# Tiles 4 and 5 of the first feed-forward turned by VectorE and through device memory, with a new order

## The chip, the cores and the metric

The program runs on one core of a Trainium2 chip. Its engines are TensorE (PE; its weight loads are shown as PEld), VectorE (DVE), ScalarE (ACT), GpSimd (POOL) and SyncE (SP, which here issues most of the transfers). The metric is the time of one execution on the device in microseconds (us).

## The reference

Attention, then two feed-forwards, all in fp32, on 4 x 576 = 2304 tokens of width 512:

```python
B, H, S, D = 4, 8, 576, 64                      # attention
scores = q @ k.T / sqrt(D), masked where (pos_q // 64) < (pos_k // 64)
attn = softmax(scores);  x = attn @ v           # heads joined: 2304 x 512
h = x @ w_in                                    # 512 -> 1024
solu = h * softmax(h)
ln = (solu - mean) / sqrt(var + 1e-6) * g_ln    # over the 1024
x = ln @ w_out                                  # 1024 -> 512
h = x @ w2_in                                   # 512 -> 2048
g = h * tanh(log1p(exp(h)))
out = g @ w2_out                                # 2048 -> 512
```

## The kernel before

All products keep fp32 accuracy by splitting each operand into a high and a low part and adding three products (high x high, high x low, low x high). L345 and L348 make a high part on ACT or POOL, L351 and L354 the low part on DVE or POOL.

**Attention** (`pair`, L639) works in 16 pairs of heads, four pairs to a batch. For a pair PE makes the scores (L792), DVE the maxima (L828, L854), ACT the exponentials with their sums (L812), POOL the division by the sum (L868, "norms": ten instructions, two heads times five blocks of queries, pt0 to pt4), PE the transposes of the result (L885), DVE and ACT the copies of these out of PSUM (L891, L894), PE the product with v (L906, L913, "pv").

**The first feed-forward** (`moe1_tile`, L951) works in 18 tiles of 128 tokens, 9 groups of two, woven between the pairs from the second batch on. POOL splits the tile's x into a high and a low part (L348, L354), with two buffers of each. PE makes h with 24 matmuls (L980), in four steps of six. DVE takes the maximum (L1005), ACT the exponentials (L1007), DVE the product (L1012), ACT the squares (L1017), POOL the layer norm (L1023, L1025) into e, of which there are three. The second product wants the tile with its 1024 features on the partitions, and there are two ways to get it:

- Plain: PE makes 8 transposes into PSUM (L1040), ACT the high part lth from PSUM (L345), DVE the low part ltl (L351).
- Turned (`moe1_turn`, L1050): DVE transposes e within blocks of 32x32 (L1060), SP stores it to device memory (L1061) and reads it back into ltl so that the blocks change places (L1064); then ACT makes lth and DVE ltl, both from SBUF.

There is one lth and one ltl, each with a half for either tile of a group. The group's second product (`moe1_x2`, L1072) is 96 matmuls (L1078), then ACT copies it out of PSUM (L1095) and SP stores it (L1098). Weights are scaled and split on the way by all engines (L469 to L527).

**The second feed-forward** (L1261 to L1522) does three groups of 768 tokens, with part of its blocks combined so that fewer products are needed (L1281, L1373, L1405), from about 390 us on.

**The order** of each engine's queue is planned when the program is built, by a list scheduler (`Plan`, L95). Every operation has an estimated cost, the operations it depends on, and a due time, which is `base + step * i` out of the table PRIO for its kind and the number of its tile or pair; an engine that is free takes the operation ready by the estimate with the lowest due time. Tiles from 6 on have due times of their own, of the names that end in "_z" (L942). The eight banks of PSUM are given out in the same plan. An entry of `ends` (L1093) makes a tile's first step of L980 wait in the plan for the second product three groups earlier.

Of the kernel before, what the change touches and what calls it, by code (L numbers as in the profile page):

```python
# [16 lines left out]
AF = mybir.ActivationFunctionType  # L17
# [22 lines left out]
    "m_x": (3584561924, 4.740681981), "m_h": (3584519723, 224.5432339), "m_v": (3578365590, -84.55132086),  # L40
    "m_w": (3584549757, 31.61235543), "m_u": (3578776343, 462337.2769), "m_s": (3583814990, 14.58923958),
    "m_l": (3584293716, 224.7120364), "m_t": (3584285833, 15.52739263), "m_e": (3584649368, -15732.34345),
    "m_2": (3584549910, 3.263592163), "m_o": (3584964114, -730.4305853),
    "store": (58386273008.57153, -19416.76233711018), "load_k_b": (2099539261, 66301361.76),
    "load_q_b": (2280296400, -83.7998511), "load_v_b": (3584392328, -36.03664193), "tr_b": (3573582281, 115.1413154),
    "te_b": (3583493493, 70.21914347000001), "sc_b": (3584300715, -653.4032456), "mx_b": (3574374210, 834066.0729),
    "ex_b": (3573775268, 127599.6585), "su_b": (3578364250, 29.19757548), "nm_b": (3584435794, 211661.1709),
    "pt_b": (3578363557, 165.0890833), "pe_b": (3584395710, -341.7218587), "pv_b": (3584415435, -2.221819743),
    "po_b": (3584391454, 26.30453126), "f_x": (58390434490.2532, 1768.025953882861),
    "f_t": (58371420326.68462, 3135.361618856386), "f_s": (3584428469.415521, 4.026125945181665),  # L50
    "f_h": (58390429881.5704, 1955.565874337728), "f_c": (3583099578.05821, 33.34836585602606),
    "f_d": (3584434386.986156, -235.5845758800226), "f_v": (58371478114.65918, 316.375216701946),
    "f_a": (58370115856.04984, 57586.70997751181), "f_pa": (58389724266.28586, 11.24711881543841),
    "f_pb": (3605493742.834323, -937869.0345814368), "f_qa": (58371450659.66384, 403.297702353877),
    "f_qb": (58371282887.06215, 12127.04963138201), "f_oa": (58380321299.68896, 492616.8487495577),
    "f_ob": (58386515692.55923, 64046.06512203981), "f_ea": (58387500502.18478, 27343.66933933209),
    "f_eb": (58389243067.357, 31275.66497336231), "f_ga": (3584428449.271045, 4.026125945181665),
    "f_gb": (58371476723.55054, 113.1749626307466), "w2c": (58392108169.53233, 419.4872966149516),
    "w2cr": (3601350414.022446, -762901.4270400213), "w2p": (3599949210.25516, -1918829.73352),
    "w2q": (58390522316.82204, -82311.19795111436), "w2br": (3588491921.201982, -390526.3022309779),  # L60
    "w2b": (58371421877.10077, 978.8919243511407), "f_p": (58385293999.53715, 95352.01411378416),
    "f_q": (3583103160.04437, 2541.501991236126), "f_o": (3583019597.915153, -19416.76233711018),
    "f_e": (3572968236.729074, 1136300.372042182), "f_b": (58383687706.18044, 5.384888595012861),
    "f_p1": (58389906945.48666, 1914.35193605864), "f_q1": (3582481840.635309, 64046.06512203981),
    "f_o1": (3582978577.934009, -22.66799827023639), "f_e1": (58390440550.8709, 33.34836585602606),
    "f_gc": (3584434234.266353, -235.5845758800226), "f_pc": (3576948007.906397, 376573.2326307783),
# [6 lines left out]
    "m_o_z": (58386217914.21704, 4407.161850113993), "m_s_z": (58391201631.55981, -768559.3758905744),
    "m_t_z": (58393876313.12167, -610611.3720098342), "m_u_z": (58383670558.39252, 1294.017841619403),
    "m_v_z": (58392113639.12505, 189.399987384369), "m_w_z": (3622369903.655326, -3465318.056893601),
    "m_x_z": (3584795119.264935, 49.97933876348363), "m_y_z": (3584428441.267128, 4.355726728622709),
}
# [224 lines left out]
def kernel(  # L302
# [58 lines left out]
    def ps(s):  # L361
        return banks[s.at // 2][:, s.at % 2, :]
# [276 lines left out]
    def pair(p, xt):  # L639
# [1028 lines left out]
```

## Time and profile before

| | us |
|---|---|
| runs | 760.08, 760.74, 761.40 |
| median | 760.74 |
| profiled execution | 761.4 |
| its span | 759.6 |
| PE busy | 749.1 |
| DVE busy | 574.4 |
| ACT busy | 443.2 |
| POOL busy | 253.3 |

The span is the time from the first to the last instruction that the profiler recorded; 1.8 us lie around it. Busy times are sums over instructions of an engine. Matmuls overlap one another, so what PE spends on a row of them is read from the start of the first to the start of the next other instruction, not from the mean duration.

### The profile page before, as it was taken

Reading aid. Unit: us, or ns where it says so; the run is one execution under the profiler, and the core shown is the slowest. Engines: PE = TensorE matmul, PEld = TensorE weight load, DVE = VectorE, ACT = ScalarE, POOL = GpSimd, SP = SyncE. Lnnn points to the kernel's source line nnn. Section 1 sums busy time; section 2 is a strip of 40 time slices with the busy share of each in tenths; the row PEclk is TensorE's granted clock in tenths of the full one; section 3 lists DMA queues with packets and bytes.
Section 4 is the critical chain, followed back from the end, with each engine's and each line's share of the span. In section 5 each row is a group of like instructions: output and inputs, shape, how many; then the busy total and the mean of one; then the engine's idle time right before and its main releaser. Section 6 shows DMA issues by size and latency. Waiting matters only on the chain.

```text
span 759.6 us, 14749 instructions
## 1 busy us (share of the span) xinstructions
PE 749.1 (99%) x5490; PEld 682.7 (90%) x5490; DVE 574.4 (76%) x1187; ACT 443.2 (58%) x936; POOL 253.3 (33%) x299
## 2 busy tenths in 40 slices
PE   8999999999999999999999999999999999999998
PEld 6888888788888899999998989989988999999998
DVE  6989888999997999978833868752334579569995
ACT  5998897686766565544723745554455555354560
POOL 2687877784674333543410242210000000000000
PEclk9999999999999999999999999999999999999999
DMA  7764653336335376658664676772287561282303
GB/s 189 181 152 106 153 129 98 98 83 171 122 115 188 98 242 197 210 186 313 243 218 163 246 263 217 251 283 99 80 291 228 169 250 59 95 302 73 98 1 111
DMA packets 114023, 128.58 MB, mean 169 GB/s; under 512 B 64160, under 2 KB 81824, under 8 KB 113952
## 3 DMA queue, kind: packets, MB, share of 16 engines
q1 hardware_dynamic: 113536, 127.35, 52.5%
q8 instruction: 43, 0.70, 0.4%
q10 hardware_dynamic: 416, 0.30, 0.1%
q14 instruction: 28, 0.23, 0.1%
HBM read 81.48 MB, written 46.14 MB: 168 GB/s over the span
## 4 chain that ended last, share of the span: by engine, by line
PE 89%; DVE 7%; ACT 2%; issue 1%; POOL 1%; DVEq 0%; ACTq 0%
PE ps L1281 23%; PE ps L1405 13%; PE ps L1078 12%; PE ps L1373 12%; PE ps L980 10%; PE ps L792 5%; PE ps L885 5%; PE ps L906 5%; PE ps L913 1%; PE ps L728 1%; DVE nmx L854 1%; DVE ltl L351 1%; PE ps L1040 1%; ACT pt L812 1%; POOL pt L868 1%
## 5 line engine op out<-in xcount | busy, mean ns | idle before, releaser
L1281 PE MATMUL ps<-wk,w2ih 128*128 128x384 f32 x576 | 146.7, 336 | 0.0
L868 POOL TENSOR_SCALAR pt<-pt,sm 128x576 f32<-128x576 f32 (+4 forms) x160 | 93.6, 605 | 32.0 <-ACT pt L812 14.1
L1281 PEld LDWEIGHTS ps<-wk,w2ih 128*128 128x128 f32 x576 | 102.7, 188 | 1.0
L980 PE MATMUL ps<-wk 128*128 128x512 f32 x432 | 103.3, 394 | 0.0
L1281 PE MATMUL ps<-wk,w2il 128*128 128x384 f32 x288 | 96.9, 336 | 0.0
L980 PEld LDWEIGHTS ps<-wk 128*128 128x128 f32 x432 | 79.6, 188 | 17.1 <-issue 1.1
L812 ACT ACTIVATE pt<-ps,nmx 128x192 f32<-128x192 f32 (+4 forms) x160 | 81.7, 525 | 20.3 <-DVE nmx L854 13.5
L1078 PE MATMUL ps<-lth,woh 128*128 128x256 f32 x288 | 82.3, 286 | 0.0
L1078 PE MATMUL ps<-ltl,woh 128*128 128x256 f32 x288 | 81.5, 283 | 0.6 <-DVE ltl L351 0.5
L1078 PE MATMUL ps<-lth,wol 128*128 128x256 f32 x288 | 81.6, 283 | 0.0
L527 POOL TENSOR_TENSOR wem<-wem 128x512 f32<-128x512 f32 x40 | 54.6, 1367 | 62.7 <-DVE wem L524 31.9
L1405 PE MATMUL ps<-w2oh,cl 128*128 128x512 f32 x144 | 56.2, 390 | 0.3 <-DVE cl L351 0.3
L1078 PEld LDWEIGHTS ps<-ltl,woh 128*128 128x128 f32 x288 | 54.3, 188 | 1.3 <-DVE ltl L351 0.7
L1373 PE MATMUL ps<-w2oh,cl 128*128 128x256 f32 x196 | 55.2, 282 | 0.0
L1078 PEld LDWEIGHTS ps<-lth,woh 128*128 128x128 f32 x288 | 54.3, 188 | 1.0 <-issue 0.5
L1078 PEld LDWEIGHTS ps<-lth,wol 128*128 128x128 f32 x288 | 54.2, 188 | 0.0
L1281 PEld LDWEIGHTS ps<-wk,w2il 128*128 128x128 f32 x288 | 54.1, 188 | 0.0
L885 PE MATMUL ps<-ident,pt 128*128 128x128 f32 (+1 forms) x400 | 51.4, 276 | 1.1 <-DVE kl L351 0.6
L885 PEld LDWEIGHTS ps<-ident,pt 128*128 128x128 f32 (+1 forms) x400 | 45.4, 142 | 6.4 <-issue 2.5
L354 POOL TENSOR_TENSOR wk<-xf,wk 128x768 fp32r<-128x768 f32 x9 | 21.1, 2339 | 71.0 <-ACT wk L345 65.7
L854 DVE TENSOR_REDUCE nmx<-ps 128x2 f32<-128x896 f32 (+1 forms) x64 | 40.7, 679 | 5.3 <-PE ps L792 3.5
L906 PE MATMUL ps<-ptw,vraw 128*64 128x256 f32 (+1 forms) x384 | 38.1, 348 | 0.0
(195 smaller groups left out, 1937.4 us busy)
## 6 DMA issues: line engine op xcount, KB each, us to landing
blk_d<-wk SPq DMA_DIRECT2D x36, 384.0 KB, 3.6
wk<-blk_d SPq DMA_DIRECT2D x36, 384.0 KB, 5.7
wraw<-in_moe_w_in_dram SPq DMA_DIRECT2D x24, 512.0 KB, 4.3
park_d<-wem SPq DMA_DIRECT2D x20, 448.0 KB, 2.8
wraw<-in_moe_w_out_dram SPq DMA_DIRECT2D x16, 512.0 KB, 4.2
wem<-park_d SPq DMA_DIRECT2D x18, 448.0 KB, 4.3
lT_d<-e SPq DMA_DIRECT2D x10, 512.0 KB, 3.2
ltl<-lT_d SPq DMA_DIRECT2D x10, 512.0 KB, 4.8
```

What stands on the lines that cost most here:

```text
L527: add(POOL, c_tt(wd), lambda: nc.gpsimd.tensor_tensor(out=mf(), in0=mf(), in1=ex().bitcast(F32), op=ALU.mult), r=[ek], w=[mk], **pt)
L792: nc.tensor.matmul(out=dst[:R1(t)], lhsT=a_[hs, (t + 1) * P - R1(t):(t + 1) * P], rhs=m_[hs, o + c0:o + c1], start=(i == 0), stop=(i == 2 ...
L812: add(ACT, c_act(EXT[t], acc=True), lambda: nc.scalar.activation(out=pp.t[0:R1(t), x * EXT[t]:(x + 1) * EXT[t]] if t < 4 else pp.t[:, x * ...
L854: add(DVE, 2 * c_dve(512), lambda s=s, ts=ts: [nc.vector.tensor_reduce(out=nmx.t[0:R1(t), :, t], in_=ps2(s)[0:R1(t), :, o:o + EXT[t]], axi ...
L868: nc.gpsimd.tensor_scalar(pp, pp, sm.t[0:R1(t), x, t:t + 1], 1.0, op0=ALU.mult, op1=ALU.mult)
L885: nc.tensor.transpose(ps2(s)[:, a, o + P - n:o + P], pts[t].t[0:n, c * P:(c + 1) * P], ident[0:n, 0:n])
L906: nc.tensor.matmul(out=ps(os_[r])[x * D:(x + 1) * D, o:o + n_], lhsT=vr.t[:, j, x, :], rhs=packs[pi].t[:, a, c0:c0 + n_], start=(i in (0, ...
L980: nc.tensor.matmul(out=ps2(hp)[:, hf, :], lhsT=x.t[:, kk, :], rhs=w[:, kk, hf * 512:(hf + 1) * 512], start=bool(first), stop=bool(last))
L1078: nc.tensor.matmul(out=ps(s)[:, (c % 2) * 256:(c % 2) * 256 + 256], lhsT=w[:, kk, cs], rhs=x.t[:, :, :, kk, :].rearrange("p o a j -> p (o ...
L1281: nc.tensor.matmul(out=ps(s)[:, 0:HT], lhsT=sl_i[j, w][:, c, a, :], rhs=x.t[:, mv], start=(start and c == 0 and i == 0), stop=(c == 1 and ...
L1373: nc.tensor.matmul(out=ps(acc[bi])[:, h * 256:(h + 1) * 256], lhsT=x.t[:, a], rhs=sl_o[j, w][:, b], start=(first and h == 0 and y == 0), s ...
L1405: nc.tensor.matmul(out=ps(acc[t]), lhsT=x.t[:, 2 * t + f], rhs=plain(j, w, f), start=(first and f == 0 and y == 0), stop=(last and f == 1 ...
```

## The change

Tiles 4 and 5, which were plain, are turned (`TURNED = range(4, 16)`), so that 12 tiles are turned and tiles 0 to 3, 16 and 17 are plain. The due times with names in "_z" hold from tile 4 on. An entry of `ends` is made from group 1 on, so that the tiles of group 4 wait in the plan for the second product of group 1. Nearly all due times from "wor" on have new numbers, of which the diff below shows one. The conditions with `p < 99` are true for every pair (p goes to 15), so with them the same copies run on the same engines.

```diff
@@ -35,45 +35,49 @@ PRIO
...
-    "wi": (3584443192, 7.799761221), "wor": (3586624350, -34.01260267), "wo": (3584561778, 29.75716834),
...
+    "wi": (3584443192, 7.799761221), "wor": (6008160774.962386, 25.39232252916657),
...
@@ -887,7 +891,7 @@
-            if pi == 1:
+            if pi == 1 and p < 99:
...
@@ -917,13 +921,13 @@
-            if r:
+            if r and p < 99:
...
-                add(ACT, c_act(w), lambda c0=c0, w=w: nc.scalar.activation(
-                    out=xt.t[:, h2, c0:c0 + w], in_=ps(os_[0])[:, 0:w], func=AF.Copy), r=[oks[0]], w=[xks[0]],
-                    rel=[os_[0]], prio=pri("po", p))
+                add(ACT, c_act(w), lambda r=r, c0=c0, w=w: nc.scalar.activation(
+                    out=xt.t[:, h2, c0:c0 + w], in_=ps(os_[r])[:, 0:w], func=AF.Copy), r=[oks[r]], w=[xks[r]],
+                    rel=[os_[r]], prio=pri("po", p))
...
@@ -940,9 +944,9 @@
     def mpri(tag, i):
-        return pri(tag + ("_z" if i >= 6 else ""), i)
-
-    TURNED = range(6, 16)
+        return pri(tag + ("_z" if i >= 4 else ""), i)
+
+    TURNED = range(4, 16)
...
@@ -1090,7 +1094,7 @@
-            if g >= 3 - 1:
+            if g >= 2 - 1:
                 ends[g] = o.seq
```

By count the new program has 48 transposes at L1040 where before has 64, 12 instead of 10 of L1060, and 12 instead of 10 of each of the transfers of L1061 and L1064; every other kind has the same number. What moves is shown below at three places. Lines of after are four higher than the same lines of before (L885 is L889, L1078 is L1082 and so on).

PE, end of the transposes of the last pair (pt0_1 is the block of queries 0 of one of its heads; ident the identity; e1, e2 tiles 4 and 5; vraw1 the pair's v). Before:

```order
L885 MATMUL ps2_65<-ident_67,pt2_1_119 128x128
L885 MATMUL ps2_65<-ident_67,pt1_1_117 128x128
L885 MATMUL ps2_65<-ident_67,pt0_1_115 128x64
L1040 MATMUL ps0_63<-ident_67,e1_147 128x128 x8
L1040 MATMUL ps3_66<-ident_67,e2_148 128x128 x8
L906 MATMUL ps1_64<-ptw0_124,vraw1_101 64x256 x2
L906 MATMUL ps1_64<-ptw1_125,vraw1_101 64x128 x2
```

After:

```order
L889 MATMUL ps1_64<-ident_67,pt3_1_121 128x128
L889 MATMUL ps1_64<-ident_67,pt2_1_119 128x128
L889 MATMUL ps1_64<-ident_67,pt1_1_117 128x128
L889 MATMUL ps1_64<-ident_67,pt0_1_115 128x64
L1082 MATMUL ps3_66<-lth0_155,woh_90 128x256
L1082 MATMUL ps3_66<-ltl0_156,woh_90 128x256
L1082 MATMUL ps3_66<-lth0_155,wol_91 128x256
```

The sixteen transposes of e1 and e2 are gone, and behind the pair's last transpose stands the second product of group 2 (lth0, ltl0) where pv stood.

ACT, what makes the high parts of tiles 4 and 5 (lth0; ptw are copies of the transposed pt out of PSUM). Before:

```order
L1095 ACTIVATE xo1_88<-ps2_65 128x512
L894 ACTIVATE ptw0_124<-ps3_66 128x1024
L894 ACTIVATE ptw2_126<-ps2_65 128x896
L345 ACTIVATE lth0_155<-ps0_63 128x8x4x32
L345 ACTIVATE lth0_155<-ps3_66 128x8x4x32
L492 ACTIVATE ps0_63<-wem1_95 128x512
L924 ACTIVATE xt1_145<-ps1_64 128x320
```

After:

```order
L816 ACTIVATE pt3_0_120,sm0_139<-ps1_64,nmx0_137 128x448 x2
L816 ACTIVATE pt0_0_114,sm0_139<-ps1_64,nmx0_137 64x64 x2
L816 ACTIVATE pt1_0_116,sm0_139<-ps3_66,nmx0_137 128x192 x2
L349 ACTIVATE lth0_155<-ltl0_156 128x1024
L816 ACTIVATE pt2_0_118,sm0_139<-ps3_66,nmx0_137 128x320
L349 ACTIVATE lth0_155<-ltl0_156 128x1024
L816 ACTIVATE pt2_0_118,sm0_139<-ps3_66,nmx0_137 128x320
L928 ACTIVATE xt1_145<-ps0_63 128x320
```

The two high parts now read ltl0 and not PSUM, and stand between the exponentials of pair 14 (pt2_0), where they stood behind the last copies of the last pair.

POOL, norms of pair 14 (pt0_0 to pt4_0) and of pair 15 (pt0_1 to pt4_1), with wk the buffers of the split x. Before:

```order
L1023 TENSOR_TENSOR st2_152<-st2_152,edges_72 128x1
L1025 TENSOR_SCALAR e0_146<-e0_146,st2_152 128x1024
L868 TENSOR_SCALAR pt4_1_123<-pt4_1_123,sm1_140 128x576 x2
L868 TENSOR_SCALAR pt3_1_121<-pt3_1_121,sm1_140 128x448 x2
L868 TENSOR_SCALAR pt2_1_119<-pt2_1_119,sm1_140 128x320 x2
L868 TENSOR_SCALAR pt1_1_117<-pt1_1_117,sm1_140 128x192 x2
L868 TENSOR_SCALAR pt0_1_115<-pt0_1_115,sm1_140 64x64 x2
L527 TENSOR_TENSOR wem1_95<-wem1_95 128x512
L348 TENSOR_SCALAR wk_89<-xt0_144 128x512
L354 TENSOR_TENSOR wk_89<-xt0_144,wk_89 128x512
```

After:

```order
L872 TENSOR_SCALAR pt0_0_114<-pt0_0_114,sm0_139 64x64 x2
L352 TENSOR_SCALAR wk_89<-xt0_144 128x512
L358 TENSOR_TENSOR wk_89<-xt0_144,wk_89 128x512
L872 TENSOR_SCALAR pt4_1_123<-pt4_1_123,sm1_140 128x576 x2
L872 TENSOR_SCALAR pt3_1_121<-pt3_1_121,sm1_140 128x448 x2
L872 TENSOR_SCALAR pt2_1_119<-pt2_1_119,sm1_140 128x320 x2
L872 TENSOR_SCALAR pt1_1_117<-pt1_1_117,sm1_140 128x192 x2
L872 TENSOR_SCALAR pt0_1_115<-pt0_1_115,sm1_140 64x64
L1027 TENSOR_TENSOR st0_150<-st0_150,edges_72 128x1
L872 TENSOR_SCALAR pt0_1_115<-pt0_1_115,sm1_140 64x64
```

The split of a tile of x (tile 10 after) now stands ahead of the norms of pair 15, and an instruction of a layer norm (st0) ahead of the last of them; before, two splits followed behind the norms and a weight product.

## Rows read from the trace of the kernel before

**Rows 1.** Head of the page: the span, busy us by engine.
```profile
span 759.6 us, 14749 instructions
...
PE 749.1 (99%) x5490; PEld 682.7 (90%) x5490; DVE 574.4 (76%) x1187; ACT 443.2 (58%) x936; POOL 253.3 (33%) x299
```

**Rows 2.** PE's waits: line, releaser, us in total, times, longest.
```profile
PE ps L728 <- ACT pt L812: 1.6, 2, 1.4
...
PE ps L1078 <- DVE ltl L351: 0.5, 1, 0.5
```

**Rows 3.** Two stretches: length, busy us of each engine, granted clock, DMA.
```profile
125.00:245.00 120.00, 119.82 (x1061) 101.64 (x1060) 110.47 (x228) 81.82 (x187) 79.76 (x102) 1.00 0.44 130
410.00:760.00 350.00, 346.06 (x2106) 328.96 (x2104) 229.76 (x519) 175.95 (x333) 26.82 (x14) 1.00 0.51 175
```

**Rows 4.** PE in time: start, us, line, operation, count, [idle before].
```profile
241.02 2.99 PE L885 MATMUL ps<-ident,pt 128*128 128x128 f32 x25
243.94 1.97 PE L1040 MATMUL ps<-ident,e 128*128 128x128 f32 x16
245.83 2.38 PE L906 MATMUL ps<-ptw,vraw 128*64 128x256 f32 x24
...
389.89 1.91 PE L1040 MATMUL ps<-ident,e 128*128 128x128 f32 x16
391.56 0.60 PE L1281 MATMUL ps<-wk,w2ih 128*128 128x384 f32 x2
```

**Rows 5.** The turned path's instructions by shape: busy us, mean ns, idle before.
```profile
L1060 DVE STREAM_TRANSPOSE e<-e 128x1024 f32<-128x1024 f32 x10 | 12.3, 1233 | 0.0
L351 DVE TENSOR_TENSOR ltl<-ltl,lth 128x1024 fp32r<-128x1024 f32 x10 | 12.2, 1248 | 0.0
...
L345 ACT ACTIVATE lth<-ltl 128x1024 fp32r<-128x1024 f32 x10 | 10.5, 1055 | 7.5 <-DMA ltl<-lT_d 7.5
```

**Rows 6.** The reads at L1064, from issue to landing.
```profile
DMA to landing us min/median/max: 3.8/4.8/6.5
```

**Rows 7.** All engines in time around the last pair's scores and norms.
```profile
225.81 0.47 PE L792 MATMUL ps<-kh,qh 64*128 64x448 f32 x2
...
227.62 2.38 PE L906 MATMUL ps<-ptw,vraw 128*64 128x256 f32 x24
...
229.95 0.63 ACT L812 ACTIVATE pt<-ps,nmx 128x448 f32<-128x448 f32 x1 [3.00 <-DVE nmx L854]
...
230.67 1.29 PE L885 MATMUL ps<-ident,pt 128*128 128x128 f32 x9
...
233.46 0.21 ACT L812 ACTIVATION_READ_ACCUMULATOR pt<-ps,nmx 128x1 f32 x1
...
234.51 6.21 POOL L868 TENSOR_SCALAR pt<-pt,sm 128x576 f32<-128x576 f32 x10 [5.19 <-ACT ptw L894]
```

**Rows 8.** Chain that ended last, in time: start, us, line, count.
```profile
333.13 11.52 PE ps L1078 x96
344.64 10.91 PE ps L980 x48
```

**Rows 9.** POOL's instructions by shape: busy us, mean ns, idle before.
```profile
L527 POOL TENSOR_TENSOR wem<-wem 128x512 f32<-128x512 f32 x40 | 54.6, 1367 | 62.7 <-DVE wem L524 31.9 <-DVE wem L512 27.6 <-DVE sm L806 2.0
...
L1023 POOL TENSOR_TENSOR st<-st,edges 128x1 f32<-128x1 f32 x18 | 12.7, 706 | 39.2 <-DVE st L1020 30.6 <-ACT pt L812 4.4 <-DVE st L1010 4.1
L348 POOL TENSOR_SCALAR wk<-xt 128x512 fp32r<-128x512 f32 x16 | 11.6, 726 | 34.1 <-PE ps L980 34.1
L868 POOL TENSOR_SCALAR pt<-pt,sm 64x64 f32<-64x64 f32 x32 | 11.0, 355 | 0.0
```

**Rows 10.** POOL in time, one split of x.
```profile
265.80 0.63 POOL L348 TENSOR_SCALAR wk<-xt 128x512 fp32r<-128x512 f32 x1
266.51 1.30 POOL L354 TENSOR_TENSOR wk<-xt,wk 128x512 fp32r<-128x512 f32 x1
```

**Rows 11.** SP's queue in time, its longest stand at issues.
```profile
401.11 6.12 SPq L1098 DMA_DIRECT2D x_d<-xo  x2
```

More of the change, by code (lines that the diff above doesn't have):

```diff
@@ L37 @@
     "pv": (3577602489, 48250.73415), "po": (3584548697, -23973.45369), "wir": (3584391592, -19.40282866),
[2 rows of a table removed]
[L40 to L66, printed above, removed]
@@ L67 @@
-    "f_qc": (58383687262.01283, 13.38236390586725), "f_oc": (58389948370.77222, 292.4769573812346),
-    "f_ec": (58391600633.60854, 28506.90281875799), "m_f": (3584285833, 15.52739263),
-    "m_g": (3584649368, -15732.34345), "m_y": (3584285833, 15.52739263),
-    "m_2_z": (3584411683.580256, 1158.898595520469), "m_e_z": (3583097759.795254, 93.04242884762695),
-    "m_f_z": (3576036552.304828, 925082.38871505), "m_g_z": (58383687409.47991, 1.493118386126717),
-    "m_h_z": (3584421142.964115, 529.2117548921229), "m_l_z": (58390132850.49834, -24266.92028098213),
@@ L73 @@
[L73 to L76, printed above, removed]
[3 rows of a table added]
+    "m_h": (4146513034.229027, 3437.496074077945), "m_v": (1685692734.528723, 70908.15921127236),
@@ new lines @@
+    "m_w": (3513359135.780956, 44.92415547201797), "m_u": (3512651070.661022, 34412.19942918024),
+    "m_s": (3602385031.112902, 229.5407375045089), "m_l": (3512621139.104277, 48.91441027733243),
+    "m_t": (3606374493.707211, 57176.39760572281), "m_e": (3784256872.698033, 46580.35398076692),
+    "m_2": (5814751679.425178, 28.5543752261172), "m_o": (4154032517.959847, 50721.31479615544),
+    "store": (3784480023.569042, 13636.80493405584), "load_k_b": (3513412592.897239, 18.28911371657496),
@@ new lines @@
+    "load_q_b": (3591457380.578043, 5455.750659667706), "load_v_b": (5814747705.540405, 37.91630800520451),
+    "tr_b": (3513512623.624942, 2488.864339361115), "te_b": (3513057446.15823, 20449.54855869562),
+    "sc_b": (3598471054.04015, -12660.51456856392), "mx_b": (4146460362.438111, 4956.416609931926),
+    "ex_b": (3513202159.696492, 278.2843291448102), "su_b": (3512973138.696665, 30410.34632864956),
+    "nm_b": (5982003734.634109, 6084678.409851378), "pt_b": (3512517669.298651, 67677.18311275712),
@@ new lines @@
+    "pe_b": (3512467939.144368, 83173.24540044068), "pv_b": (3606497905.709489, 90.00238067856172),
+    "po_b": (3513385991.199829, 26.56050018958916), "f_x": (6008156650.597215, 779.5970689903637),
+    "f_t": (3512610350.138847, 297.2943001073333), "f_s": (3513379921.223451, 4443.91599878809),
+    "f_h": (4154435668.646057, 4366.717098724009), "f_c": (3512037548.931818, 110873.3650727735),
+    "f_d": (3589689352.875807, 100987.1606545643), "f_v": (3513530414.556408, 161.5853800552079),
+    "f_a": (3598525495.763744, 170280.8380340209), "f_pa": (6034878513.585733, -14655.90053063708),
@@ new lines @@
+    "f_pb": (3602385031.112902, 229.5407375045089), "f_qa": (3842060795.519964, 530797.0666234276),
+    "f_qb": (3784481313.98589, 13636.80493405584), "f_oa": (-34603326918.33231, 1916686514.745709),
+    "f_ob": (3512607912.105052, 515.2284187708756), "f_ea": (4148351975.506439, 251384.4518498256),
+    "f_eb": (3513326696.170582, 293.7535488451618), "f_ga": (-4661520550.137727, -21372.20211791259),
+    "f_gb": (3602413546.967874, 149.3463499252079), "w2c": (6008154478.291977, 699.1231476218337),
@@ new lines @@
+    "w2cr": (3513152301.192077, 12933.16787216247), "w2p": (3512786932.347193, 43329.16647657341),
+    "w2q": (4146479428.070339, 278.1596871225091), "w2br": (3513354402.041589, 185.2169332069646),
+    "w2b": (3513357920.996052, 2648.217017198866), "f_p": (3784450968.790502, 5197.830628909945),
+    "f_q": (6008153046.339516, 897.8736645491898), "f_o": (3513194028.87609, 26801.98206807588),
+    "f_e": (6008160178.324902, 229.5407375045089), "f_b": (3513404899.396112, 16.29491305222635),
+    "f_p1": (5814751385.815626, 24.38853313023387), "f_q1": (3511641561.398437, 104369.5322552285),
@@ new lines @@
+    "f_o1": (3602283256.191959, 1416131.234380976), "f_e1": (3512914070.688581, -21774.17885624363),
+    "f_gc": (3512409399.332546, -37.78460661017908), "f_pc": (5814751203.764366, 37.88205393319141),
+    "f_qc": (3513354402.041589, 185.2169332069646), "f_oc": (3591426039.129261, 6190.879925856177),
+    "f_ec": (6034648267.007865, 95.66622213876178), "m_f": (3584285833, 15.52739263),
+    "m_g": (3584649368, -15732.34345), "m_y": (3584285833, 15.52739263),
+    "m_2_z": (4142659699.299991, 284285.4825035536), "m_e_z": (3512611608.553393, 574.706807828762),
@@ new lines @@
+    "m_f_z": (1685692385.457383, 70908.27551583681), "m_g_z": (3512574052.685516, 6014.459998772267),
+    "m_h_z": (5814751173.256117, 38.1373011500683), "m_l_z": (4154203218.34231, 29332.82787552609),
+    "m_o_z": (5806522791.316294, 630850.4569228797), "m_s_z": (3511815669.800803, 85067.1320595883),
+    "m_t_z": (3605651132.16607, 52408.33006597407), "m_u_z": (3854040242.696799, 1540.748222960061),
+    "m_v_z": (4167864452.473848, 75.48390070549195), "m_w_z": (3513270665.232864, 38393.04278283695),
@@ L77 @@
+    "m_x_z": (3784923448.291461, 625.3016034869008), "m_y_z": (3512553666.470055, 361.3495936685188),
 }
```

3 rows, old and new, of the table PRIO are left out of this document.

## The prediction

> **What bounds the kernel now.** I began with the page's head: TensorE (PE) is busy 749.1 of a span of 759.6 us [rows 1]. A busy PE can still wait between matmuls, so next came PE's waits: the longest that belongs to the first feed-forward is 0.5 us, the largest group of all 1.6 us [rows 2]. Then the stretches: between 125 and 245 us, where tiles 4 and 5 are worked beside the last attention pairs, PE is busy 119.8 of 120 us, VectorE (DVE) 110.5 and GpSimd (POOL) 79.8 at full granted clock; after 410 us the second feed-forward has PE at 346.1 of 350 and DVE at 229.8 [rows 3]. So the time is the number of matmuls in PE's queue, and an edit pays what it takes out of that queue, less the waits it puts in. The other engines matter where a result comes just in time.
>
> The profiled execution took 761.4 us (759.6 of span, 1.8 around it); the median of the runs shown is 760.74. I work with differences against the profiled one and take them off the median.
>
> **Part 1: the transposes that go.** Sixteen of PE's 64 transposes at L1040 belong to tiles 4 and 5. The trace has just these 16: they start at 243.94 and the next matmuls at 245.83, so 1.89 us, of which 0.15 is the change to another kind of matmul; 16 others took 389.89 to 391.56, 1.67 us; and the 25 transposes ahead of the first lot took 2.92 us, 0.117 each [rows 4]. I take 16 x 0.109 = **-1.74** (bounds -1.67 and -1.89). None of it lies beside other PE work.
> The Trainium skill speaks against the edit here: in "VectorE: DVE Perf Modes", section "The three transpose paths", TensorE is the path to use for 128x128 when the result may lie in PSUM, at 390 ns each. By that price 16 would be 6.2 us (an estimate from that page) and the time 754.5; the rows price all 16 in a row, so they decide.
>
> **Part 2: what replaces them.** Per tile: one DVE transpose of 1.23 us, one store and one read of 512 KB, a high part on ScalarE (ACT) of 1.06 us and a low part on DVE of 1.25, where the old path has the same two parts from PSUM [rows 5]. So only the DVE transposes and the transfers are new: DVE has 9.5 us to spare in the stretch and gets 2.5 more. The reads land 3.8 to 6.5 us after issue [rows 6]. They may start only when the product of group 1 (tiles 2, 3) is done, because there is one pair of buffers lth, ltl. Call that moment zero. PE's new queue has from there to the product of group 2: scores of 24 matmuls, pv, 6 of L980, 8 transposes, 12 of L980, 17 transposes. Scores take 1.81 and pv 3.05 [rows 7]; a matmul of L980 is 10.91/48 = 0.227 and one of L1078 11.52/96 = 0.120 [rows 8]. The sum is 1.81 + 3.05 + 1.36 + 0.87 + 2.72 + 1.85 = 11.7 us. The second read, issued 0.4 after the first, lands by 6.9 at the worst of the rows; 1.06 and 1.25 later all is ready, at 9.2. So I cost the round trip at nothing, with 2.5 us of cover (bounds 0 to 1: a stretched DVE instruction and one softmax exponential on ACT first do not use the cover up). What is queued behind the wait: on ACT, which now stands at the first lth in the middle of pair 14's exponentials, one exponential, the second lth and another exponential; pair 14's sums and POOL's norms wait for those. PE's next transposes of that pair come 11.7 + 1.44 + 1.0 + 4.32 = 18.5 us after zero (12 products, a half run of scores, 36 products). The norms end about 15.4: the second lth at 8.0, an exponential and the sums to 9.2 (1.2 is an estimate), ten norms in 6.21 [rows 7].
>
> **Part 3: the order of the last pair.** Here I see a cost. Before, the last pair's scores end at 227.62, the exponentials run from 229.95 to 233.67, POOL's ten norms 234.51 to 240.72, PE's transposes start at 241.02 [rows 7]: 13.4 us of cover, all but 0.3 used. After, PE has between the same two points pv, 6 of L980, 9 transposes, 12 of L1078, pv, 12 of L1078: 3.05 + 1.36 + 1.0 + 1.44 + 3.05 + 1.44 = 11.3 us, and the last 9 of the 25 transposes follow 1.8 later, at 13.1. And POOL now stands ahead of the norms at tile 10's splits (L348, L354 of before), which write a buffer that tile 8's last 6 matmuls read: L348 is the line that waits 34.1 us for L980 in the trace [rows 9]. Those 6 end at 3.05 + 1.36 = 4.4. With 0.2 for the signal (an estimate), 0.71 and 1.30 for the splits [rows 10], nine norms of the ten in 6.21 - 0.36 = 5.85, L1023's 0.71 that stands ahead of the tenth, and that tenth, 0.36 [rows 9]: the last norm ends near 13.5. PE's last nine want it at 13.1, and notice is 0.1. Cost **+0.5** (bounds 0, if the splits start half a microsecond sooner, and 1.2, if L1023 also waits for its DVE chain). The exponentials can hardly be the later of the two: run as before right behind the scores they end near 5, before the splits do.
> Pair 13 has the same pattern: PE wants eight norms at 6.2 after zero, and POOL has before them a weight product (L527, 1.37) that waits for DVE until about -1.5, two splits and seven of the eight norms: -1.5 + 1.37 + 0.71 + 1.30 + 7 x 0.62 gives 6.2, and the signal on top. The -1.5 is an estimate: DVE has some eight instructions of about half a microsecond between pair 13's last exponential and it. Cost **+0.1**, bounds 0 and 0.9.
> One run of scores more than before (32 for 31), by the 0.15 of a change of kind: **+0.15**, bounds 0 and 0.3.
>
> **Part 4: the rest.** Groups 3 and 4 get 54 and 66 matmuls of L980 between products where before had 48 (12.3 and 15.0 us for 10.9); the later groups keep 48, under which the trace shows one wait of 0.5 [rows 2]. Group 3's low parts need the same 9.2 us and have weight work of ACT and DVE in front of them, which no row shows in this order; 12.3 leaves it 3.1. The stretch with the transposes of tiles 16 and 17 keeps its order, so its 0.5 stays. The second feed-forward has the same instructions in a slightly different weave with DVE free a third of the time. Zero for all of it, bounds -0.5 (the one wait goes) and +0.7. The `p < 99` branches change nothing: p ends at 15.
>
> Sum: -1.74 + 0.5 + 0.1 + 0.15 = **-1.0**, so 760.4 against the profiled execution and **759.7** against the median. A difference under 0.2% (1.5 us: outside 759.2 to 762.3) is more than a measurement of this kernel can tell from no change, and 759.7 is inside.
>
> **Rivals.**
> A, all new waits are hidden. For it: before, pair 15's norms were 0.3 us early and PE did not wait [rows 7], and its longest wait in the first feed-forward was 0.5 [rows 2]. Against it: the two POOL places above come out late by the trace's own durations. Then -1.74 + 0.15, and up to half of that 0.5 gone as well: 758.9 to 759.2.
> B, POOL is the bound of the last pairs and gives everything back: the two places at their upper bounds, 1.2 + 0.9, and 0.15: +0.5, so 761.2. For it: POOL is two thirds busy with norms, splits and weight products in one queue. Against it: in the trace its queue is empty for 5 us ahead of the last pair's norms [rows 7].
> C, slower: the read back for group 2 is issued late and ACT stands in front of the exponentials. Its place is SP's queue: the two reads stand behind a load of a weight chunk that waits for DVE to free its buffer. SP can stand 6.1 us at two issues [rows 11]. Cover is 2.5 us; with the issue 6 us late, PE waits 3.5 for the product (the pair behind it, whose exponentials stood on ACT, is then 6 late with 3.1 of spare and the same 3.5): -1.74 + 3.5 + 0.75 of the other terms = +2.5, so 763.2. It decides from an issue 5 us late. Against it: that load's buffer is freed by an instruction that comes out at -1.5, ahead of zero.
> D, the edit takes out nothing, since PE would have waited in those 1.7 us anyway: before, PE had no wait on either side of the 16 [rows 4], so I leave it a rest.
>
> **How the numbers follow.** Forecast with waits of 0.3 to 1.5: 0.42, no measurable change. A: 0.37, faster. B and D: 0.10, no change. C and other waits of over 3 us: 0.11, slower. So faster 0.37, same 0.52, slower 0.11. The likeliest case alone spans 759.2 to 760.6. For 8 in 10 I go down to 758.3 (the sixteen at 1.89 and all of the 0.5 gone) and up to 762.2, by the upper bounds of Parts 1, 3 and 4: -1.67 + 1.2 + 0.9 + 0.3 + 0.7 = +1.4.
>
> **What would show it.** L1040 x48 and L1060 x12 with the same means (Part 1). ACT's waits for the reads of ltl, between exponentials, and PE without a wait at the first product matmul of group 2 (Part 2). PE waiting 0.3 to 0.8 us at L885's line for POOL in the last pair, POOL's L348 starting right after the 6 of L980 (Part 3). No new wait on PE after 410 us (Part 4). I would be wrong by the size if PE's waits in the stretch add to under 0.2 or over 2.5; wrong in kind if PE waits for a DMA.

## The result, and the profile after

The changed kernel takes **765.38 us** (median of 9 runs, 764.56 to 769.97) against 761.05 of the kernel before beside it (9 runs, 760.02 to 764.89): a ratio (of the means) of 1.007, with a 95% interval of 1.0044 to 1.0095. It is slower by 0.7%. Forecast were 759.7 and a range up to 762.2: wrong in sign and outside the range. Six of after's runs took 764.56 to 766.44 us and three 769.15 to 769.97; none of the three was profiled, so what they lose stays open.

The profiled execution of after took 764.56 us. The head of its page, to be read beside [rows 1]:

```profile
span 762.6 us, 14746 instructions
...
PE 747.3 (98%) x5474; PEld 678.5 (89%) x5474; DVE 576.6 (76%) x1189; ACT 444.2 (58%) x936; POOL 250.6 (33%) x299
```

PE is busy 1.8 us less, as the sixteen transposes are gone, and yet the span is 3.0 us longer. So PE waits more. The stretches say where; columns as in [rows 3], first before, in three pieces, of which the prediction read only the first two, as one sum:

```profile
125.00:185.00 60.00, 59.90 (x524) 49.23 (x522) 56.15 (x120) 44.93 (x107) 39.54 (x47) 1.00 0.39 104
185.00:245.00 60.00, 59.92 (x537) 52.41 (x538) 54.31 (x109) 36.89 (x82) 40.23 (x55) 1.00 0.49 155
245.00:310.00 65.00, 65.00 (x413) 57.40 (x412) 60.70 (x111) 37.65 (x57) 22.36 (x25) 1.00 0.57 184
```

and after:

```profile
125.00:185.00 60.00, 55.67 (x460) 45.84 (x459) 55.15 (x113) 40.82 (x90) 42.49 (x46) 1.00 0.41 112
185.00:245.00 60.00, 59.69 (x475) 51.58 (x474) 54.97 (x110) 36.87 (x79) 35.97 (x50) 1.00 0.59 186
245.00:310.00 65.00, 65.00 (x500) 56.80 (x501) 49.55 (x96) 37.44 (x68) 21.99 (x30) 1.00 0.47 155
```

PE stands idle 4.33 us between 125 and 185 us (0.10 before), 0.31 in the next 60 (0.08). DVE, which was fullest after 245 us (60.70 of 65), is there down to 49.55: the new order has spread DVE's work otherwise, and PE's waits have gone to an earlier place. PE's waits of after between 120 and 260 us, as in [rows 2]; before had in this stretch a single one, of 0.2 us, at L728:

```profile
PE ps L732 <- ACT pt L816: 1.6, 2, 0.9
PE ps L796 <- ACT pt L816: 1.1, 1, 1.1
PE ps L984 <- ACT pt L816: 0.9, 1, 0.9
PE ps L1044 <- POOL e L1029: 0.5, 1, 0.5
PE ps L889 <- DVE e L1016: 0.2, 1, 0.2
```

The first three groups, 3.6 us of 4.3, wait for softmax exponentials (L816), which free the PSUM bank that PE wants next: transposes of a new pair (L732), scores (L796), a step of the first feed-forward (L984). They belong to pairs 10 to 12; the prediction had weighed pairs 13 and 15.

Why the exponentials are late is in DVE's queue. A pair's scores come in three lots (three groups of blocks of queries, each with its PSUM banks), and DVE takes the maxima of each lot before ACT can work on it. After, from the first lot of maxima of pair 11 to the first lot of pair 12 (L858 maxima; L472, L474, L516, L528, L550 pieces of w_out; L925 the copy of pair 9's product with v):

```profile
148.94 1.28 DVE L858 TENSOR_REDUCE nmx<-ps 128x2 f32<-128x896 f32 x2
150.15 0.73 DVE L550 SCALAR_TENSOR_TENSOR wol<-wem,g_sb,woh 128x512 fp32r<-128x512 f32 x1
150.81 0.68 DVE L516 SCALAR_TENSOR_TENSOR wem<-wraw,wem 128x512 f32<-128x512 uint32 x1
151.41 0.68 DVE L528 SCALAR_TENSOR_TENSOR wem<-wraw,wem 128x512 int32<-128x512 int32 x1
152.01 0.41 DVE L472 TENSOR_SCALAR wem<-wraw 128x512 int32<-128x512 int32 x1
152.34 0.41 DVE L474 TENSOR_SCALAR wem<-wraw 128x512 int32<-128x512 int32 x1
152.68 0.41 DVE L925 COPY xt<-ps 128x256 f32<-128x256 f32 x1
153.12 0.42 DVE L855 MEMSET ps<- 64x128 f32 x2
153.57 1.29 DVE L858 TENSOR_REDUCE nmx<-ps 128x2 f32<-128x384 f32 x2
...
158.22 0.41 DVE L474 TENSOR_SCALAR wem<-wraw 128x512 int32<-128x512 int32 x1
158.56 1.27 DVE L858 TENSOR_REDUCE nmx<-ps 128x2 f32<-128x896 f32 x2
```

and before, the same two lots of a pair:

```profile
146.91 1.27 DVE L854 TENSOR_REDUCE nmx<-ps 128x2 f32<-128x896 f32 x2
148.20 0.42 DVE L851 MEMSET ps<- 64x128 f32 x2
148.54 0.67 DVE L546 SCALAR_TENSOR_TENSOR wol<-wem,g_sb,woh 128x512 fp32r<-128x512 f32 x1
149.13 1.27 DVE L854 TENSOR_REDUCE nmx<-ps 128x2 f32<-128x384 f32 x2
```

From the first lot of pair 11 to its second it is 4.6 us after and 2.2 before: five pieces of weights and a copy stand between where one piece stood. And on PE the scores of the next pair come sooner:

```profile
148.88 0.31 PE L796 MATMUL ps<-kl,qh 64*128 64x320 f32 x2
...
154.65 0.52 PE L796 MATMUL ps<-kh,qh 64*128 64x448 f32 x2
...
156.88 0.36 PE L796 MATMUL ps<-kh,qh 64*128 64x192 f32 x2 [1.15 <-ACT pt L816]
```

Pair 12's scores begin 5.5 us after pair 11's are done at 149.12 (before, two such lots lay 16.7 us apart, from 145.73 to 162.39), and its second lot stands 1.15 us for a bank of pair 11.

By the starts of matmuls the account is: tile 0's first step of L980 (L984) starts at 109.58 before and 107.93 after, the product of group 6, when the same work is done, at 355.39 and 357.58. Between the two after takes 3.8 us more with 1.74 us less to do, so it loses 5.6 us. Of these, 4.5 are idle time of the two stretches above; part of the rest is that a wait costs more by the starts of matmuls than its idle time (from 125.78 to 128.14 after needs 2.36 us for what takes before 1.47, from 127.42 to 128.89: 0.89 for a wait shown as 0.73). What follows adds 0.8 (0.31 of it a wait of PE for ACT at 443.57 us), and the quicker start, of which more below, takes off 1.65: 3.0 in all.

### The profile page after: what moved, and what is told of

Its sections match the earlier page's. It is cut to its first block, busy times and chain, and to the rows that moved or that the text cites. A ratio compares the mean times of both kernels' runs of the same rounds, so it can differ in the third digit from the quotient of the medians.

```text
span 762.6 us, 14746 instructions
## 1 busy us (share of the span) xinstructions
PE 747.3 (98%) x5474; PEld 678.5 (89%) x5474; DVE 576.6 (76%) x1189; ACT 444.2 (58%) x936; POOL 250.6 (33%) x299
## 4 chain that ended last, share of the span: by engine, by line
PE 81%; DVE 10%; ACT 3%; POOL 2%; DMA 2%; issue 1%; SPq 0%; DVEq 0%; ACTq 0%; POOLq 0%
PE ps L1285 23%; PE ps L1409 12%; PE ps L1377 12%; PE ps L1082 11%; PE ps L984 10%; PE ps L796 4%; PE ps L889 4%; PE ps L910 4%; DVE nmx L858 2%; POOL pt L872 1%; ACT pt L816 1%; PE ps L917 1%; DVE e L1016 1%; DVE wem L474 1%; DVE st L1009 1%
## 5 line engine op out<-in xcount | busy, mean ns | idle before, releaser
L984 PE MATMUL ps<-wk 128*128 128x512 f32 x432 | 103.9, 394 | 1.1 <-ACT pt L816 0.9
L872 POOL TENSOR_SCALAR pt<-pt,sm 128x192 f32<-128x192 f32 (+4 forms) x160 | 92.4, 599 | 34.7 <-ACT pt L816 13.2
L816 ACT ACTIVATE pt<-ps,nmx 128x576 f32<-128x576 f32 (+4 forms) x160 | 81.9, 527 | 24.1 <-DVE nmx L858 12.6
L984 PEld LDWEIGHTS ps<-wk 128*128 128x128 f32 x432 | 79.5, 188 | 18.0 <-ACT pt L816 1.3
L531 POOL TENSOR_TENSOR wem<-wem 128x512 f32<-128x512 f32 x40 | 54.4, 1359 | 87.2 <-DVE wem L528 63.0
L1082 PE MATMUL ps<-lth,woh 128*128 128x256 f32 x288 | 82.9, 288 | 0.0
L1082 PE MATMUL ps<-ltl,woh 128*128 128x256 f32 x288 | 81.3, 282 | 0.5 <-DVE ltl L355 0.5
L1082 PE MATMUL ps<-lth,wol 128*128 128x256 f32 x288 | 81.7, 284 | 0.0
L1082 PEld LDWEIGHTS ps<-lth,woh 128*128 128x128 f32 x288 | 54.2, 188 | 1.4 <-issue 0.7
L1082 PEld LDWEIGHTS ps<-ltl,woh 128*128 128x128 f32 x288 | 54.2, 188 | 0.9 <-DVE ltl L355 0.7
L1082 PEld LDWEIGHTS ps<-lth,wol 128*128 128x128 f32 x288 | 54.3, 188 | 0.0
L889 PE MATMUL ps<-ident,pt 128*128 128x128 f32 (+1 forms) x400 | 51.0, 274 | 1.4 <-DVE kl L355 0.6
L889 PEld LDWEIGHTS ps<-ident,pt 128*128 128x128 f32 (+1 forms) x400 | 44.7, 141 | 7.4 <-issue 3.0
L858 DVE TENSOR_REDUCE nmx<-ps 128x2 f32<-128x896 f32 (+1 forms) x64 | 40.9, 681 | 4.7 <-PE ps L796 3.3
L526 ACT ACTIVATE wem<-wem,edges 128x512 int32<-128x512 int32 x40 | 29.0, 724 | 18.9 <-DVE wem L472 18.8
```

Source lines behind the costliest of these rows:

```text
L531: add(POOL, c_tt(wd), lambda: nc.gpsimd.tensor_tensor(out=mf(), in0=mf(), in1=ex().bitcast(F32), op=ALU.mult), r=[ek], w=[mk], **pt)
L816: add(ACT, c_act(EXT[t], acc=True), lambda: nc.scalar.activation(out=pp.t[0:R1(t), x * EXT[t]:(x + 1) * EXT[t]] if t < 4 else pp.t[:, x * ...
L858: add(DVE, 2 * c_dve(512), lambda s=s, ts=ts: [nc.vector.tensor_reduce(out=nmx.t[0:R1(t), :, t], in_=ps2(s)[0:R1(t), :, o:o + EXT[t]], axi ...
L872: nc.gpsimd.tensor_scalar(pp, pp, sm.t[0:R1(t), x, t:t + 1], 1.0, op0=ALU.mult, op1=ALU.mult)
L889: nc.tensor.transpose(ps2(s)[:, a, o + P - n:o + P], pts[t].t[0:n, c * P:(c + 1) * P], ident[0:n, 0:n])
L984: nc.tensor.matmul(out=ps2(hp)[:, hf, :], lhsT=x.t[:, kk, :], rhs=w[:, kk, hf * 512:(hf + 1) * 512], start=bool(first), stop=bool(last))
```

## Experiments

Kernels whose diff shows a SKIP do not issue the instructions of the operations listed in it, so their tiles hold stale data; their order is otherwise that of the kernel named. Line numbers of all of them are shifted by what was added.

### Fewer weight pieces on VectorE

Ten instructions (L516, L528 of w_out chunks 3 to 7; 6.8 us) left out of either kernel.

```diff
         for o in order:
-            o.fn()
+            if o.seq not in SKIP:      # 10 operations of "wo"
+                o.fn()
```

> The changed kernel in its own order, but ten VectorE instructions are not issued: the two combining steps (low mantissa bits, sign) of the w_out chunks 3 to 7, 6.8 us of VectorE work that stood between 131 and 168 us. Theory D (VectorE is full in the stretch 125 to 185, the softmax maxima stand behind the weight work, so exponentials and with them PSUM banks come late): PE's waits there, some 6 us now, fall below 2.5, and the time to 761 to 762 from 765. Rival P (the waits come from PE's own new order, scores of two pairs close together, whatever VectorE does): waits and time stay, 764.5 to 765.5.

> The same ten VectorE instructions not issued in the kernel before, as a control. Theory D: PE is busy 59.9 of 60 us in the stretch, so there is nothing to win: 760.5 to 761.1. Rival (those instructions cost time everywhere, by their power, port or memory traffic): 1 to 3 us less here too.

Measured: after without them 761.57 (760.87 to 762.64; ratio to before 1.0013, 1.0003 to 1.0022), 3.8 us less than after; before without them 759.05 (0.9983, 0.9973 to 0.9992), 1.5 less than before. The same ten instructions are worth 2.3 us more in the new order (by medians; the intervals of after with and without them don't touch): DVE is what is short there. PE's idle time between 125 and 185 us fell from 4.33 to 2.12, as theory D had it. The control missed: theory D had nothing to win there, and the 1.5 us are in the range of its rival, so a part of DVE's work costs time in the old order too. The waits of after that begin at 138 and 167 us went, those at 127, 155 and 160 stayed (0.77, 0.78 and 0.56 us of idle time).

### The sixteen transposes alone, and the turn in the old order

Before, with the sixteen transposes of tiles 4 and 5 not issued; and a kernel with the whole work in which those tiles are turned, while every instruction that before has keeps its place in its queue, and new ones stand where they are ready.

```diff
-    TURNED = range(6, 16)
+    TURNED = range(4, 16)
...
-    order = plan.order()
+    order = plan.order([list(ranges(t)) for t in WANT])   # before's queues, engine by engine
```

> The kernel before with the sixteen PE transposes of tiles 4 and 5 not issued and nothing in their place (the copies read what the banks hold). By the prediction's Part 1 this is worth 1.74 us: 759.3. Rival: the sixteen covered the copies of the last pair's transposes (ScalarE's last ends 244.96, PE's transposes of the pair 243.94), so PE waits 1.2 us before the product with v, and VectorE, busy 60.7 of 65 us behind it, gives little back: 760.3 to 761.0.

> Tiles 4 and 5 turned, while every other instruction of every engine stays in the order of the kernel before; the new instructions stand where their inputs are ready. Theory O (the new order alone costs the time): 759.3, by 1.74 less than before. Theory D (VectorE is nearly full from 125 to 310 us, so two transposes and two later low parts there push its other work, and PE waits for it behind 245 us): 762 to 766, no better than the changed kernel by more than 3.

Measured: 762.9 (761.68 to 763.43; ratio 1.0023, 1.0008 to 1.0037) and 765.83 (765.46 to 766.02; 1.0066, 1.0051 to 1.0081). Taking 1.74 us of work out of PE made the kernel slower by 1.7 us (by the ratio), where the expectation had 1.74 less and its rival no change: both missed. The turned kernel came out as theory D had it. The longest wait and two stretches of the first kernel, the next matmuls behind the wait among them:

```profile
PE ps L1081 <- DVE ltl L354: 2.6, 2, 2.1
```

```profile
284.00:288.00 4.00, 1.90 (x12) 1.47 (x11) 4.00 (x6) 1.20 (x2) 3.36 (x3) 1.00 0.81 201
288.00:292.00 4.00, 4.00 (x23) 4.00 (x22) 3.97 (x8) 1.47 (x2) 0.90 (x2) 0.57 0.50 195
```

The low parts of group 3 on DVE, in before and without the sixteen:

```profile
285.17 2.35 DVE L351 TENSOR_TENSOR ltl<-ltl,lth 128x1024 fp32r<-128x1024 f32 x2
```

```profile
284.61 2.55 DVE L354 TENSOR_TENSOR ltl<-ltl,lth 128x1024 fp32r<-128x1024 f32 x2
```

In before PE comes to the product of group 3 at 287.77, 0.25 us after the low parts are done: that was all there was in hand. Without the sixteen it comes at 284.84, and the low parts are done at 287.16. DVE is without a gap there and sets the time. (This profile started 1.5 us sooner than that of before, by tile 0's first step, so in like time PE is 1.4 us earlier and DVE 1.1 later. DVE's delay is in two instructions that took longer beside POOL's splits of x: L1214 2.10 us at 252.16 where before has 1.01, L471 1.20 at 257.92.) PE waits 2.1 us, and then the granted clock is 0.57 of full over 4 us: the level of 1.2 GHz for 3.4 us, one matmul each 0.21 us and no longer 0.12, some 1.5 us lost. In the turned kernel the same wait is longer (3.4 us) and so is the low level:

```profile
PE ps L1219 <- DVE ltl L492: 3.9, 2, 3.4
```

```profile
290.00:294.00 4.00, 3.67 (x17) 3.67 (x18) 3.97 (x11) 1.47 (x2) 0.00 (x0) 0.50 0.66 252
```

Its DVE has 2.5 us more work, and it also stands for the read back. The new high and low parts have the places of the old ones (L486, L492), and the data lands later than the old transposes did:

```profile
246.65 1.06 ACT L486 ACTIVATE lth<-ltl 128x1024 fp32r<-128x1024 f32 x1 [1.41 <-DMA ltl<-lT_d]
247.74 1.23 DVE L492 TENSOR_TENSOR ltl<-ltl,lth 128x1024 fp32r<-128x1024 f32 x1 [2.92 <-ACT lth L486]
```

DVE is idle for 2.92 us there (1.60 in before, for the old high part), with all its later work behind it in the queue, and the low parts of group 3 end at 290.3. So in the old order the round trip is not hidden while DVE has its whole work. Two shorter waits of PE, 0.94 us before 183.85 (for exponentials) and 0.34 before 193.32, are part of its loss too.

### The same with VectorE free

44 instructions less on DVE (31 us: pieces of w_out and of the second feed-forward's weights) in four kernels: before, after, before without the sixteen, and the turn in the old order.

```diff
-            o.fn()
+            if o.seq not in SKIP:      # 44 operations of VectorE
+                o.fn()
```

> VectorE made free: in the kernel before, 44 VectorE instructions between about 100 and 285 us are not issued, the two combining steps (low mantissa bits, sign) of 22 weight chunks, at 0.69 to 0.73 us each some 31 us. It is the base for the next three. Theory D (PE and VectorE are about equally full there): 758 to 759.3, no more than with ten left out (759.05), since PE is the bound once VectorE has room. Rival (VectorE holds PE up all along): 755 or less.

> The same 44 instructions not issued in the changed kernel. Theory D: with VectorE free the waits of 125 to 185 us go (under 1.5 us in all) and the transposes saved count: 0.5 to 2 us below the kernel before with the same left out, 757 to 758.5. Rival P (PE's new order itself costs): it stays 2 to 4 us above that one, 761 to 763.

> The kernel before without the sixteen transposes and without the 44 VectorE instructions. Theory D: the 2.1 us that PE waited for the low parts of group 3 and the half clock behind it go, and the sixteen are worth 1.2 to 1.7 less than the same without them: 757 to 758. Rival (that wait comes from the read back or from ScalarE): 2 us or more of it stay, and it is slower than the base, as it was with all of VectorE's work.

> Tiles 4 and 5 turned in the old order, without the 44 VectorE instructions. Theory D: 757 to 758.5 in place of 765.8, so the turn then gains about a microsecond on its base. Rival: it stays 2 us or more above its base, since the turn's place in the old order costs for another reason.

Measured: before 759.08 (ratio to before 0.9983, 0.9972 to 0.9993), after 760.37 (1.0001, 0.9986 to 1.0016), without the sixteen 758.03 (0.9965, 0.9956 to 0.9975), turned in the old order **757.44** (0.9962, 0.9951 to 0.9973). With DVE free the turn gains 759.08 - 757.44 = 1.64 us, close to Part 1's 1.74, and PE has no new wait: transfers and high parts are hidden then. Leaving the sixteen out gains 1.05, less than the 1.2 to 1.7 expected. Each of the two differences has an uncertainty of about 1 us. The new order is 1.3 us behind the old even so (the intervals overlap, and neither theory's range has 760.37), and 2.9 behind the old order turned, which is clear of noise: its waits at 127, 155 and 160 us (idle time 0.69, 0.78, 0.57) are still there.

### DVE work added to before

Before with e of tiles 4 and 5 transposed twice on VectorE on top of all its work (4.9 us, and the second undoes the first).

```diff
+            for _ in range(2 if i in (4, 5) else 0):
+                nc.vector.transpose(both(e.t), both(e.t))
```

> The kernel before with VectorE work added: e of tiles 4 and 5 is transposed in place twice, and so comes back as it was, 4 x 1.23 = 4.9 us in the stretch 125 to 245, where PE's work stays as it was. By the prediction VectorE has 9.5 us to spare there, so 760.5 to 761.5. Theory D (that spare is an average; the maxima and low parts that PE waits for stand in VectorE's queue behind whatever is added): 763 to 766.

Measured: 767.27 (766.16 to 768.98; ratio 1.009, 1.0071 to 1.0108), so 6.6 us for 4.9 us of work, above theory D's range. The waits are where DVE's copies and PSUM banks come late, not at the low parts, and behind the longest of them, which ends at 170.26, the granted clock is 0.68 over the 4 us from 170:

```profile
PE ps L885 <- DVE xt L921: 2.3, 1, 2.3
PE ps L1082 <- ACT pt L812: 1.7, 1, 1.7
PE ps L792 <- DVE xt L921: 1.5, 1, 1.5
```

### What holds the three waits that stayed

After with DVE free as above, and 18 first steps of w_out (L472, L474 on DVE, L526 on ACT, chunks 2 to 7) left out too.

```diff
+            if o.seq not in SKIP:      # the 44, and 18 more of "wo"
+                o.fn()
```

> The changed kernel without the 44 VectorE instructions of the run before, and also without the first steps (two on VectorE, one on ScalarE) of the w_out chunks 2 to 7, 18 instructions, 0.41 to 0.72 us each. What is left open is why the changed kernel kept waits of 0.9, 1.0 and 0.8 us at 127, 155 and 160 us when VectorE was free. If the softmax of pairs 10 to 12 stands behind those weight steps in the queues of VectorE and ScalarE, the three fall to under 0.5 in all and the time to 757.5 to 758.8. If PE's own order is the reason (the scores of pair 12 come too soon after those of pair 11, whose banks are not yet read), 1.5 or more of the 2.6 stays, and 759.3 to 760.5.

Measured: 759.25 (758.1 to 762.26; ratio 0.9985, 0.9972 to 0.9997), between the two forecasts. The waits at 127 and 160 us are gone; the one at 155 stays, the only one of PE between 120 and 200 us:

```profile
PE ps L799 <- ACT pt L819: 0.8, 1, 0.8
```

DVE's queue there, with nearly all weight pieces out of it (L928 is the copy, L861 the maxima):

```profile
152.54 0.42 DVE L928 COPY xt<-ps 128x256 f32<-128x256 f32 x1 [1.44 <-PE ps L920]
152.98 0.42 DVE L858 MEMSET ps<- 64x128 f32 x2
153.44 1.29 DVE L861 TENSOR_REDUCE nmx<-ps 128x2 f32<-128x384 f32 x2
```

DVE stands idle 1.44 us at the copy, for pair 9's product with v, while the scores of pair 11 behind it have been ready since 149.4. So this wait is made by the order of DVE's queue, not by a lack of time.

### The maxima moved ahead, with the whole work

After, with 14 weight pieces moved behind the maxima of pairs 10 to 12 on DVE; and the same with the second lot of scores of pair 12 behind the product with v.

```diff
+MOVES = (
+    (DVE, [102, 103], 945), (DVE, [122, 124, 129, 130], 1011), (DVE, [131, 133, 138, 139], 1166),
+    (DVE, [140, 142, 1504, 136], 1173),
+    (PE, [1171], 980),                 # the second kernel alone
+)
```

A line names an engine, the operations that are moved, and the one that they are put behind.

> The changed kernel with its whole work; only VectorE's queue differs: at four places between 124 and 166 us the weight pieces (two, four, four and four instructions) stand behind the softmax maxima of pairs 10 to 12 and no longer ahead of them. Theory 1 (the order of VectorE's queue makes the maxima late): the waits of the changed kernel at 127.0, 155.5, 160.7 and 167.1 us, 4.4 us together, go by more than half, and the time is 762.0 (761.0 to 763.3). Theory 2 (VectorE simply lacks time between 125 and 185 us, and what is put back is missed by the next weight piece, copy or product): the waits go elsewhere and the time stays at 765 (764 to 766.5).

> The same, and in TensorE's queue the second lot of scores of pair 12 stands behind the product with v of pair 10 and not ahead of it. Theory 1: the wait at 155.5 us, which stayed without the weight pieces, goes as well, and the time is 0.3 to 1.2 us under that of the run with the maxima alone. Theory 2: no difference, or a later wait for the exponentials of pair 12 that takes it back.

Measured: 770.49 (770.31 to 770.73; ratio 1.0123, 1.0106 to 1.014) and 772.56 (772.16 to 776.28; 1.016, 1.0135 to 1.0185). Both miss theory 1 by far, and come out worse than theory 2. The second kernel has the same wait of 4.0 us, now at the product with v. ACT's queue in the first shows why (L538 a step of the weights, L828 the exponentials):

```profile
157.50 0.72 ACT L538 ACTIVATE wem<-wem,edges 128x512 int32<-128x512 int32 x1 [3.32 <-DVE wem L484]
158.62 0.72 ACT L560 ACTIVATE woh<-wem,g_sb 128x512 fp32r<-128x512 f32 x1 [0.40 <-POOL wem L543]
159.25 0.40 ACT L828 ACTIVATE pt<-ps,nmx 128x192 f32<-128x192 f32 x1
```

The pieces that I moved back on DVE feed a step on ACT that kept its place ahead of the exponentials. ACT stood 3.3 us at it, the exponentials ran from 159.25 though their maxima were done by 155.9, PE waited 4.0 us, and its clock fell again:

```profile
PE ps L808 <- ACT pt L828: 4.0, 1, 4.0
```

```profile
160.00:164.00 4.00, 2.79 (x18) 2.08 (x20) 3.98 (x9) 3.06 (x9) 0.98 (x2) 0.50 0.31 66
```

So that the queues of DVE and ACT are tied to each other is shown; that the maxima ahead, with ACT's steps moved along, would win the time back is not. And in DVE's own queue the move won little: the second lot of pair 11 started 4.1 us after its scores' last matmul (150.55 to 154.63), where after has 4.5, since the copy of pair 9 still stood before it. No full version faster than before was found: what is faster here leaves weight work out.

## Why the prediction was wrong, point by point

**Part 1, the transposes**: the count and the price hold. 48 of L1044 are left, 0.272 us long each (they overlap), and no matmul waits where the sixteen of [rows 4] stood; with DVE free the turn is worth 1.64 us. The Trainium skill ("VectorE: DVE Perf Modes", section "The three transpose paths") has 390 ns for a 128x128 transpose in bf16, by which the sixteen, which are in f32, would have been 6.2 us, an estimate; no run here shows that, and the measurement decides. The sentence that failed is the one the price was used with, "an edit pays what it takes out of that queue": without the sixteen, and nothing else changed, the kernel is 1.7 us slower, because a later product then waits for DVE (2.1 us) and the clock goes down behind it. That was rival D's idea, that the time is not PE's to give, at a place 40 us later than the rival looked for it.

**Part 2, the round trip**: right for this order. The operations by shape as in [rows 5], and the landing as in [rows 6]:

```profile
L1064 DVE STREAM_TRANSPOSE e<-e 128x1024 f32<-128x1024 f32 x12 | 14.7, 1231 | 0.0
L349 ACT ACTIVATE lth<-ltl 128x1024 fp32r<-128x1024 f32 x12 | 12.7, 1057 | 5.5 <-DMA ltl<-lT_d 5.5
```

```profile
DMA to landing us min/median/max: 3.8/5.3/6.7
```

The two high parts run between pair 14's exponentials, at 235.88 and 237.33, and PE starts the product of group 2 at 242.22 without a wait. Rival C (SP late) did not come about. The order is part of this: in the old one the same read back made DVE stand 2.92 us. What failed here is half a sentence: "DVE has 9.5 us to spare in the stretch". That is an average over 120 us, and it isn't free at the moment when PE needs a result: 4.9 us of DVE work added to before in just that stretch cost 6.6.

**Part 3, the last pairs**: the +0.5 was 0, and pair 13's +0.1 as well. POOL's queue at the last pair, priced from [rows 7, 9, 10]:

```profile
257.24 0.62 POOL L352 TENSOR_SCALAR wk<-xt 128x512 fp32r<-128x512 f32 x1 [11.82 <-PE ps L984]
257.94 1.27 POOL L358 TENSOR_TENSOR wk<-xt,wk 128x512 fp32r<-128x512 f32 x1
259.67 4.79 POOL L872 TENSOR_SCALAR pt<-pt,sm 128x576 f32<-128x576 f32 x9 [0.45 <-ACT ptw L898]
264.43 0.55 POOL L1027 TENSOR_TENSOR st<-st,edges 128x1 f32<-128x1 f32 x1
264.96 0.32 POOL L872 TENSOR_SCALAR pt<-pt,sm 64x64 f32<-64x64 f32 x1
```

The splits do start as soon as the six of L984 let them, as forecast, but the norms took 4.8 us for nine (5.85 expected) and L1027 0.55, so PE began its 25 transposes at 264.83 and never stood: rival A, at this place. The +0.15 for one more run of scores is priced by no run. The step that decided is not in Part 3 at all: it priced the new order at pairs 13 and 15, where I had looked, and put the new order at pairs 10 to 12 at nothing, without a reason. There the scores came closer together, weight pieces came to stand ahead of maxima, and PE waited 4.3 us.

**Part 4, the rest**: what comes behind the product of group 6 costs 0.8 more (bound for all of Part 4: 0.7), with a wait for ACT at 443.57 us that before has not, and "zero for all of it" left the stretch of 245 to 310 us unread, where DVE was busy 60.70 of 65 us. That row says what bounded that part of before: DVE and PE at once. From it a rival would have come that the prediction lacks: DVE is the second bound, and each microsecond put on it costs one (-1.7 + 2.5 and more).

In sum: the turn itself is worth -1.7 on PE; turned in the old order, the 2.5 us of DVE work, DVE's stand for the read back and the low clock make it 5.0 slower net; the new order avoids the wait at 285 us and pays 5.6 ahead of it instead, between 125 and 245. Ten DVE pieces account for 3.8 of these (2.3 above what they are worth in before), two waits of 0.6 to 0.8 us (127, 160) go with the weight steps on DVE and ACT, and one (155) is the order's own. These are differences of separate runs and do not add up exactly. Which due time of the new table brought the scores forward was not tried, nor was the new table with tiles 4 and 5 plain; so what the table would cost without the turn is not shown.

## What to carry to other kernels

Before you credit an edit with the work that it takes off the fullest engine, read every stretch behind it for a second engine that is as full there: the edit is worth only what that engine's queue can follow. If a new order comes with the edit, go through the queues of the engines that feed the bottleneck over the whole region that moved, and ask of every result that PE needs what now stands ahead of it in its in-order queue; busy shares don't show that. Moving one instruction back by hand moves the wait to the engine that takes its result, unless that partner moves too.

## What the runs showed of the hardware

- A wait of PE of 2.1 us was followed by 3.4 us at 1.2 GHz (0.57 granted over 4 us), one of 2.3 by 0.68 over 4 us, those of 3.4 and 4.0 by 0.50 over 4 us, and in the turned kernel 0.79 over the next 4. The clock stayed at 1.00 behind the waits of 0.5 to 1.2 us in after and behind those of 1.5 and 1.7 in before with the DVE work added. So the wait of 2.1 us cost about 1.5 us more than its length.
- Some DVE instructions are stretched, ahead of the waits at 127 and 167 us too: L474 took 1.51 us at 124.79, L550 1.78 at 163.40, where their medians are 0.42 and 0.79. Both began while POOL ran L531 (124.57 to 126.03 and 163.22 to 164.63) and ended 0.3 and 0.55 us after it. The Trainium skill ("SBUF — State Buffer", section "Who interferes with whom") lets certain instructions of these two engines run only one after the other, the later one blocked; both places agree with that, and so do two where POOL came second (L531 at 152.17 and 158.04 took 1.74 and 1.73 us for 1.29, and DVE's L474 beside it 0.41). No run here tries it.
- The profiles start in two ways, though the work is the same up to tile 0's first step: in before the granted clock is 0.97 over the first 60 us and that step comes at 109.58, in after it is 1.00 and 107.93, 1.65 us sooner. So the two spans understate the difference by 1.6 us.
